# First parameter load ahead of the gate weights, a fixed VectorE order in the head, one engine per transpose copy, and the column matmuls ahead of tile 2

## The chip, the cores and the metric

The kernel runs on one NeuronCore of one Trainium2 chip. The metric is device time in microseconds; the time of a kernel is the median of its runs. The engines are TensorE (PE), VectorE (DVE), ScalarE (ACT), GpSimd (POOL) and SyncE (SP); SP and ACT also issue the DMAs. The trace calls SP's DMA queue q1 and ACT's q10.

## The reference

One layer on x of 2048 tokens by 448 features, in bf16. It normalizes each token, sends the result through a diagonal complex state-space scan (branch A) and a gated MLP (branch B), and joins the two:

```python
xn = _layernorm(x, axis=-1)
# branch A: dt = exp(log_dt); Lam_bar = exp(dt*Lam); B_bar = ((Lam_bar-1)/Lam)[:,None]*B
#   Bu = xn @ B_bar.T ; h_t = Lam_bar*h_{t-1} + Bu_t ; s = 2*Re(h @ C.T) + xn*Dskip
# branch B: (sigmoid(xn @ w_gate) * (xn @ w_up)) @ w_down, w_gate and w_up 448 x 1792
return x + s * silu(branch_B)
```

Lambda_re, Lambda_im and log_dt are vectors of 448; they are called "the parameters" below.

## The kernel before, in words

**Tiling.** The 2048 tokens are 16 tiles of 128, worked in four chunks of 512 tokens. The features stay on the partitions: `xnT` holds a chunk of the normalized x transposed, as 7 blocks of 64 features by 512 tokens. For each chunk, 14 steps (`gu_step`, L683) make 7 gate and 7 up blocks. In chunk 0 the seven gate blocks come first and then the seven up blocks, and from chunk 1 on they alternate. The matmuls of a step (L662, L663) go in pairs on the two halves of the array. ACT takes tanh of a gate block (L676), and DVE multiplies it with the up block (L679) into `hF`. `b_units` (L692) makes the scan's input, `ssm_pair` and `ssm_stack` (L753, L789) do the scan on DVE, `down` (L823) is the second MLP matmul, and `yout` (L841) is the scan's output matmul with the last three DVE operations (L861, L863, L865) and the store.

**The head.** The work of chunk 0 that the change touches is this. x tiles 0 to 3 are loaded one by one, tiles 0 and 2 from SP and 1 and 3 from ACT (L372 to L375). The gate weights come as four transfers. The first 256 columns of each half (blocks 0 and 1; 224 KB each) go out at L376 on SP and L377 on ACT, and the other 640 columns (blocks 2 to 6; 560 KB each) at L382 on SP and L379 on ACT. Below they are "the small" and "the large" gate-weight transfers. The three parameter rows (`load_p`, 0.9 KB each) go out on SP between them (L378, L380, L381). Then SP loads x tiles 4 to 7 in one transfer (L383), half of the up weights (L895), the skip row `dbc` (L896) and the transposed B matrices (L601).

For tiles 0 to 3, DVE computes statistics (`stats`, L395, L396), ACT the square root (L404), POOL a copy of the mean (L405), and DVE the reciprocal (L406) and the normalized tile (`norm`, L418). PE transposes each tile into a PSUM bank (`pe_transpose`, L450 to L452). For tiles 0 and 1 the bank is copied out by ACT (4 of 7 blocks, L455) and DVE (3 blocks, L457) together, and for tiles 2 and 3 by DVE alone (L460). `columns` (L486) turns the three parameter rows into columns with five small matmuls (L492, L494), DVE copies them out (`pv`, L498), and POOL works out `turn` and `r` from them (L506 to L515). The sine tables (`tables`, L522) start from `turn`. On PE the head runs: 11 warm-up matmuls, transposes of tiles 0 and 1, two warm-up matmuls, gate block 0 of tiles 0 and 1, transposes of tile 2, gate block 1 of tiles 0 and 1, transposes of tile 3, the columns, then gate block 2 of tiles 0 and 1. That last one needs both large transfers.

**What sets the order.** Operations are not issued as written. `Plan.add` (L82) records each with an engine, a cost and its dependencies. `Plan.solve` (L132) works out a latest start for each backwards from PE's written order, and then runs all engines forward, taking on each engine the ready operation with the earliest latest start; `emit` (L222) writes the instructions in the order of the planned starts. PE operations keep the written order (L102), and so do DMAs and others added with `chain=True`. DVE, ACT and POOL operations may change places whenever a cost or a planned time changes, anywhere in the kernel. A fixed order of 16 tiles in four chunks thus comes out of the costs that are written in the code.

**The DMA counters.** The DMAs from SP and ACT take eight completion counters in turn, and a DMA that reuses a counter waits at issue until the DMA eight places before it has landed. The planner has the same rule:

```python
k = len(landed)
if k >= 8:
    o.end = free[e] = max(o.end, landed[k - 8] + o.cost)
```

In the issued order of the kernel before, the large SP gate-weight transfer is the eleventh DMA and the small one on SP the third. So the large one waits for the small one to land, and the instructions after it in SP's queue wait behind it. The large one on ACT is the tenth and waits for x tile 2, the second.

Of the kernel before, what the change touches and what calls it, by code (L numbers as in the profile page):

```python
# [20 lines left out]
P = 128  # L21
H = 64
# [50 lines left out]
class Plan:  # L73
# [3 lines left out]
    def __init__(self, horizon):  # L77
        self.ops, self.w, self.r = [], {}, {}
        self.horizon = horizon
        self.last_of = {}  # L80

    def add(self, eng, cost, fn, r=(), w=(), dma=0, lat=None, chain=False, name="", rate=230e3):  # L82
# [19 lines left out]
        if chain or eng == "PE":  # L102
# [29 lines left out]
    def solve(self, pe_from):  # L132
# [58 lines left out]
        while todo:  # L191
# [13 lines left out]
            if o.dma:  # L205
                if e == "POOL":
                    o.lat = 6.0
                else:
# [3 lines left out]
                    q = dma_free[e] = max(dma_free.get(e, 0.0), o.end + 1.2) + o.dma / o.rate  # L212
                    o.lat = q + 0.8 - o.end
# [14 lines left out]
def kernel(  # L228
# [113 lines left out]
    def load_w(eng, k, half, b, r=()):  # L342
# [5 lines left out]
             wsrc[k][:, c0 + m0 * P:c0 + m1 * P].rearrange("(s p) f -> p s f", p=H), cost=0.65, r=r, rate=145e3)  # L348
# [26 lines left out]
    load_x(3, 1, "ACT")  # L375
    load_w("SP", "g", 0, 0)  # L376
    load_w("ACT", "g", 1, 0)  # L377
    load_p("SP", 0)  # L378
    load_w("ACT", "g", 1, 1)  # L379
    load_p("SP", 1)  # L380
# [12 lines left out]
    def stats(t):  # L393
        b = t % 3
        add("DVE", 0.53, lambda: V.bn_stats(out=bst[b][:], in_=x_all[:, t, :]), r=[("x", t)], w=[("bst", b)])  # L395
        add("DVE", 0.1, lambda: V.bn_aggr(out=mv[:, t, :], in_=bst[b][:]), r=[("bst", b)], w=[("mv", t)])  # L396

    def chain(t0, n):
# [4 lines left out]
        if t0 < TPC:  # L403
            add("ACT", 0.2, lambda: A.activation(sd, var, ACT.Sqrt, bias=epsc[:]), r=ks("mv") + ["sqrttab", "epsc"], w=ks("sd"))  # L404
            add("POOL", 0.15, lambda: G.tensor_copy(out=meanf[:, t0:t0 + n, :], in_=mean), r=ks("mv"), w=ks("mf"))  # L405
            add("DVE", 0.09, lambda: V.reciprocal(out=rs, in_=sd), r=ks("sd"), w=ks("rs"))  # L406
# [8 lines left out]
    def norm(t):  # L415
        b = t % NXN
        if t < TPC:
            add("DVE", 0.33, lambda: V.tensor_scalar(out=xn[b][:, 0:448], in0=x_all[:, t, :],  # L418
# [25 lines left out]
    def pe_transpose(t):  # L444
# [9 lines left out]
        if t < 2:  # L454
            add("ACT", 0.5, lambda: A.copy(out=xnT[0][:, 0:4, js], in_=tp[:, 0:4, :]),  # L455
                r=[("acc", a)], w=[("xnT", 0, t, "a")])
            add("DVE", 0.27, lambda: V.tensor_copy(out=xnT[0][:, 4:7, js], in_=tp[:, 4:7, :]),  # L457
                r=[("acc", a)], w=[("xnT", 0, t, "b")])
        else:
            add("DVE", 0.53, lambda: V.tensor_copy(out=xnT[0][:, :, js], in_=tp[:, :, :]),  # L460
# [419 lines left out]
    for t in range(4):  # L880
        stats(t)
        chain(t, 1)
        norm(t)
    slots0 = [next_gu() for _ in range(3)]

    pe_transpose(0)
    pe_transpose(1)
    warm_mm(2)
    gu_mm(0, "g", 0, slots0[0], 0, 2, True)
    pe_transpose(2)  # L890
    gu_mm(0, "g", 1, slots0[1], 0, 2, True)
# [147 lines left out]
```

## Time and profile before

| | |
|---|---|
| runs | 195.15, 193.25, 196.12, 196.08, 193.71 us; median 195.15 us |
| profiled execution | 195.15 us, of which the span of the trace is 193.4 us |
| busy, share of span | PE 94%, DVE 88%, ACT 44%, POOL 18% |
| DMA | 13.41 MB; 5.9 to 9.9 tenths busy in the first five slices, little afterwards |
| first gate matmul | 7.49 us; gate block 2 of tiles 0 and 1 starts at 13.72 us |
| mean granted PE clock | 0.987 over the span |

Times in the profile are counted from the start of the span. A PE that is shown busy need not be at its peak, since ends of matmuls are modelled. An engine's "idle before" and the waits name what came last before an instruction could start. The page's second part cuts the span into 40 slices of 4.83 us. In the row PEclk a 9 stands for the full clock.

### The profile page before, as it was taken

What the parts mean: (1) busy time and instruction counts of PE and PEld (TensorE: products, weight loads), DVE (VectorE), ACT (ScalarE), POOL (GpSimd) and SP (SyncE); (2) the same over time, 40 slices, a digit from 0 to 9 for tenths busy, and PEclk for the clock granted to TensorE, in tenths of its full rate; (3) what the DMA queues carried; (4) which work ended last, traced back from release to release, by engine and by line L of the source; (5) the groups of instructions that cost most, each with busy time, mean ns of one, the idle gap of its engine ahead of it and who ended that gap; (6) DMA issues with size and microseconds to landing.
All of it is one profiled execution on the core that took longest, in us unless ns stands there. A gap on an engine that the chain in (4) does not pass through costs nothing.

```text
span 193.4 us, 3453 instructions
## 1 busy us (share of the span) xinstructions
PE 181.2 (94%) x1340; PEld 87.5 (45%) x1347; DVE 170.3 (88%) x310; ACT 84.4 (44%) x117; POOL 34.1 (18%) x92
## 2 busy tenths in 40 slices
PE   7759999999999999999989999999989999999990
PEld 2447444444445444454435444444435444455550
DVE  3827879999999999999999999999999999992074
ACT  3515996473967835134477321244346151112100
POOL 3136583400002670000355200000000000000000
PEclk9996999999999999999999999999999999999998
DMA  5999934599300024200013410000001000101011
GB/s 143 221 237 283 166 73 98 123 333 185 124 0 3 0 47 90 56 0 0 3 29 92 96 26 24 0 27 0 24 0 51 0 0 0 54 24 47 0 42 53
DMA packets 28310, 13.41 MB, mean 69 GB/s; under 512 B 19587, under 2 KB 28294, under 8 KB 28294
## 3 DMA queue, kind: packets, MB, share of 16 engines
q1 hardware_dynamic: 26614, 11.36, 25.8%
q10 hardware_dynamic: 1680, 1.84, 3.9%
q8 instruction: 10, 0.16, 0.4%
q14 instruction: 6, 0.05, 0.1%
HBM read 6.77 MB, written 1.84 MB: 44 GB/s over the span
## 4 chain that ended last, share of the span: by engine, by line
DVE 55%; PE 28%; issue 7%; DMA 6%; POOL 2%; ACT 1%; SPq 0%; DVEq 0%; POOLq 0%
DVE hF L679 13%; PE gu L662 13%; DVE wv L769 8%; DMA wG<-in_B_w_gate_dram 6%; PE gu L830 5%; PE acc L855 4%; PE acc L830 4%; DVE ta L762 3%; DVE tb L763 3%; DVE z L765 3%; DVE o_t L861 3%; DVE tb L784 3%; DVE ta L783 3%; DVE hT L786 2%; DVE o_t L863 2%
## 5 line engine op out<-in xcount | busy, mean ns | idle before, releaser
L662 PE MATMUL gu<-xnT,wG 64*128 64x512 bf16 (+1 forms) x217 | 48.0, 367 | 2.2 <-DMA wG<-in_B_w_gate_dram 2.1
L663 PE MATMUL gu<-xnT,wG 64*128 64x512 bf16 (+1 forms) x217 | 48.0, 367 | 0.0
L662 PE MATMUL gu<-xnT,wU 64*128 64x512 bf16 x196 | 46.1, 376 | 0.0
L663 PE MATMUL gu<-xnT,wU 64*128 64x512 bf16 x196 | 46.1, 376 | 0.0
L676 ACT ACTIVATE sig<-gu 128x1024 f32<-128x1024 f32 x21 | 21.5, 1023 | 36.7 <-PE gu L663 36.5
L830 PE MATMUL acc<-wd,hF 128*128 128x448 bf16 x168 | 33.8, 353 | 0.0
L662 PEld LDWEIGHTS <-wG 64*128 64x128 bf16 x217 | 20.6, 98 | 24.8 <-issue 2.6
L830 PEld LDWEIGHTS <-hF 128*128 128x128 bf16 x224 | 21.5, 98 | 21.3 <-issue 2.1
L662 PEld LDWEIGHTS <-wU 64*128 64x128 bf16 x196 | 18.0, 94 | 23.6 <-issue 2.1
L679 DVE SCALAR_TENSOR_TENSOR hF<-sig,gu 128x1024 bf16<-128x1024 f32 x21 | 25.3, 1207 | 0.0
L769 DVE TENSOR_TENSOR_SCAN wv<-c_r,st,z 128x512 bf16<-128x512 f32 x18 | 23.0, 1276 | 0.0
L855 PE MATMUL acc<-cT,hT 128*128 128x448 bf16 x105 | 21.8, 353 | 0.0
L663 PEld LDWEIGHTS <-wG 64*128 64x128 bf16 x217 | 20.5, 98 | 0.3 <-issue 0.2
L663 PEld LDWEIGHTS <-wU 64*128 64x128 bf16 x196 | 18.0, 94 | 0.0
L726 ACT CAST bus<-gu 128x1024 bf16<-128x1024 f32 x12 | 12.1, 1011 | 12.8 <-PE gu L715 12.8
L861 DVE TENSOR_TENSOR o_t<-acc,xd 128x448 bf16<-128x448 f32 x15 | 9.2, 614 | 9.2 <-PE acc L855 9.2
L715 PE MATMUL gu<-xnT,bT 128*128 128x512 bf16 x65 | 15.3, 379 | 1.1 <-issue 1.1
L855 PEld LDWEIGHTS <-hT 128*128 128x128 bf16 x119 | 11.5, 98 | 10.1 <-issue 0.4
L836 ACT ACTIVATE g_t<-acc 128x448 bf16<-128x448 f32 x12 | 6.4, 537 | 18.3 <-PE acc L830 18.3
L395 DVE BATCH_NORM_STATS2 bst<-x_all 128x6 f32<-128x448 bf16 x16 | 9.4, 614 | 5.5 <-DMA x_all<-in_A_x_dram 5.5
L409 POOL TENSOR_SCALAR veb<-mv 128x2 bf16<-128x2 bf16 x6 | 2.5, 410 | 49.7 <-DVE mv L396 49.5
L830 PE MATMUL gu<-wd,hF 128*128 128x448 bf16 x56 | 10.8, 352 | 0.0
(131 smaller groups left out, 242.2 us busy)
## 6 DMA issues: line engine op xcount, KB each, us to landing
out_dram<-o_t SPq DMA_DIRECT2D x15, 112.0 KB, 1.7
wd<-in_B_w_down_dram SPq DMA_DIRECT2D x1, 1568.0 KB, 7.3
x_all<-in_A_x_dram SPq DMA_DIRECT2D x3, 448.0 KB, 6.5
wU<-in_B_w_up_dram SPq DMA_DIRECT2D x1, 784.0 KB, 12.4
wU<-in_B_w_up_dram ACTq DMA_DIRECT2D x1, 784.0 KB, 13.3
wG<-in_B_w_gate_dram ACTq DMA_DIRECT2D x1, 560.0 KB, 6.1
wG<-in_B_w_gate_dram SPq DMA_DIRECT2D x1, 560.0 KB, 7.3
xnT<-xn SPq DMA_TRANSPOSE x24, 2.4
```

The costliest lines, as they stand in the source:

```text
L395: add("DVE", 0.53, lambda: V.bn_stats(out=bst[b][:], in_=x_all[:, t, :]), r=[("x", t)], w=[("bst", b)])
L662: T.matmul(gu[a][:, 0, ts], lhsT=w_[0:H, s, ms], rhs=x[0:H, s, ts], start=(s == 0), stop=(s == 6))
L663: T.matmul(gu[a][:, 1, ts], lhsT=w_[H:P, (s + 1) % 7, ms], rhs=x[H:P, s, ts], start=(s == 0), stop=(s == 6))
L676: add("ACT", act(1024), lambda: A.activation(th, gu[a][:], ACT.Tanh, scale=0.5), r=[("gu", a)], w=[tk])
L679: add("DVE", dve1(1024), lambda: V.scalar_tensor_tensor(out=ho, in0=th, scalar=1.0, in1=gu[a][:], op0=ALU.add, op1=ALU.mult), r=[("gu", a) ...
L715: T.matmul(gu[a][:, i, :], lhsT=bT[:, kt, i, pt * P:pt * P + P], rhs=x[:, 2 * kt, :], start=False, stop=(kt == 2))
L726: add("ACT", act(1024), lambda u=u, a=a: A.copy(out=bus[u][:], in_=gu[a][:]), r=[("gu", a)], w=[("bus", u)])
L769: dve(1.194, lambda k=k: V.tensor_tensor_scan(out=wv[:, k, :], data0=rb, data1=z[:, k, :], initial=(st[pt][:, k, :] if c else 0.0), op0=AL ...
L830: T.matmul(d, lhsT=hF[c % 2][:, m, h, js], rhs=wd[:, ft, :], start=(ft == 0), stop=(ft == FT - 1))
L836: add("ACT", act(448), lambda: A.activation(g_t[g][:], d, ACT.Silu, scale=0.5), r=[key, "silutab"], w=[("gt", g)])
L855: T.matmul(y, lhsT=hT[c % 2][:, hm, js], rhs=cT[:, cm, c0:c1], start=(i == 0), stop=(i == 6))
L861: add("DVE", dve1(n), lambda od=od, y=y, c0=c0, c1=c1: V.tensor_tensor(out=od, in0=y, in1=xq[:, c0:c1], op=ALU.add), r=[key, ("xd", q)], w ...
```

## The change

It has six parts.

1. The first parameter row's load is moved on SP ahead of the small gate-weight transfer. On each queue the other loads keep their order. In the issued order of the changed kernel the parameter row is the third DMA, the small SP gate-weight transfer is the fifth, and the large one is still the eleventh. Its counter is now that of the parameter row. The up weights on SP now wait for the small gate weights, and `dbc` for the small ACT transfer.
2. While `pl.seq` is set, from the first statistics to the `dbc` load, DVE operations are chained in written order.
3. That written order is: statistics of tiles 0 and 1, reciprocal and norm of 0 and of 1, statistics of 2, copy of tile 1, statistics of 3, reciprocal and norm of 2 and of 3, `pv`, copies of tiles 2 and 3.
4. Tile 0's transpose is copied out whole by ACT, tile 1's whole by DVE. One ACT instruction and one DVE instruction fewer remain, each longer.
5. On PE, gate block 1 of tiles 0 and 1 and then the columns come before the transposes of tile 2.
6. Costs in the planner change: DMA latencies 1.2 to 0.9 and 0.8 to 0.6 us, the gate-weight rate 145 to 135 GB/s, and DVE and ACT costs of the head's operations upwards.

As a consequence of the last, the order on DVE, ACT and POOL changes in many places after the head too. On DVE, the first reads of PSUM of about eight `yout` steps (L861) stand one to four places earlier, and updates L679, scans L769 and table operations trade places with neighbours. On POOL, three operations of `coeffs` (L564, L570, L564) come before the first `veb` (L409). PE's order changes only in the head, and SP's by the parameter row and one swap of a transposing DMA.

```diff
@@ Plan.__init__
         self.last_of = {}
+        self.seq = False
@@ Plan.add
-        if chain or eng == "PE":
+        if chain or eng == "PE" or (eng == "DVE" and self.seq):
@@ Plan.solve
-                    q = dma_free[e] = max(dma_free.get(e, 0.0), o.end + 1.2) + o.dma / o.rate
-                    o.lat = q + 0.8 - o.end
+                    q = dma_free[e] = max(dma_free.get(e, 0.0), o.end + 0.9) + o.dma / o.rate
+                    o.lat = q + 0.6 - o.end
@@ load_w
-             ... cost=0.65, r=r, rate=145e3)
+             ... cost=0.65, r=r, rate=135e3)
@@ loads
     load_x(3, 1, "ACT")
+    load_p("SP", 0)
+    load_w("ACT", "g", 1, 0)
     load_w("SP", "g", 0, 0)
-    load_w("ACT", "g", 1, 0)
-    load_p("SP", 0)
+    load_p("SP", 1)
     load_w("ACT", "g", 1, 1)
-    load_p("SP", 1)
     load_p("SP", 2)
     load_w("SP", "g", 0, 1)
     load_x(4, 4)
@@ stats, chain, norm: costs only
-0.53, 0.1 (bn_stats, bn_aggr); 0.2 (Sqrt), 0.09 (reciprocal), 0.33 (norm)
+0.6, 0.16; 0.3, 0.2, 0.42
@@ pe_transpose
-        if t < 2:
-            add("ACT", 0.5, lambda: A.copy(out=xnT[0][:, 0:4, js], in_=tp[:, 0:4, :]), ...)
-            add("DVE", 0.27, lambda: V.tensor_copy(out=xnT[0][:, 4:7, js], in_=tp[:, 4:7, :]), ...)
+        if t == 0:
+            add("ACT", 0.85, lambda: A.copy(out=xnT[0][:, :, js], in_=tp[:, :, :]), ...)
         else:
-            add("DVE", 0.53, lambda: V.tensor_copy(out=xnT[0][:, :, js], in_=tp[:, :, :]), ...)
+            add("DVE", 0.64, lambda: V.tensor_copy(out=xnT[0][:, :, js], in_=tp[:, :, :]), ...)
@@ the head
     warm_mm(11)
-    for t in range(4):
-        stats(t)
+    pl.seq = True
+    stats(0)
+    stats(1)
+    for t in (0, 1):
         chain(t, 1)
         norm(t)
+    stats(2)
     slots0 = [next_gu() for _ in range(3)]
     pe_transpose(0)
     pe_transpose(1)
+    stats(3)
+    for t in (2, 3):
+        chain(t, 1)
+        norm(t)
     warm_mm(2)
     gu_mm(0, "g", 0, slots0[0], 0, 2, True)
+    gu_mm(0, "g", 1, slots0[1], 0, 2, True)
+    columns()
     pe_transpose(2)
-    gu_mm(0, "g", 1, slots0[1], 0, 2, True)
     pe_transpose(3)
     silu_table()
     load_w("ACT", "u", 1, 0, r=["silutab"])
     load_w("SP", "u", 0, 0)
     load("SP", "dbc", P * D * 2, dbc[:], A_Dskip.unsqueeze(0).to_broadcast((P, D)))
-    columns()
+    pl.seq = False
```

## The prediction

> **What bounds the kernel now.** I read the chain of waits first. It begins with two DMAs, one behind the other, and only then comes to an engine (columns: start, duration, what):
>
> ```profile
> 0.72 0.39 SPq L333
> 1.17 0.42 SPq L333
> 1.63 4.72 DMA wG<-in_B_w_gate_dram
> 6.37 7.31 DMA wG<-in_B_w_gate_dram
> 13.72 0.28 PE gu L662
> ```
>
> The small gate-weight transfer on SP lands at 1.63 + 4.72 = 6.35 us; the large one is issued at 6.37, lands at 13.68, and gate block 2 starts at 13.72. SP's own waits show why it went out so late:
>
> ```profile
> SPq L333 <- DMA wG<-in_B_w_gate_dram: 2.8, 1, 2.8
> ```
>
> SP was done with its fifth DMA at 3.27 + 0.25 = 3.52 and then stood for 2.8 us until the small transfer had landed: the wait for a completion counter. The waits of the compute engines from 0 to 30 us name the victims (columns: total, times, longest):
>
> ```profile
> DVE bst L395 <- DMA x_all<-in_A_x_dram: 5.5, 2, 3.4
> PE gu L662 <- DMA wG<-in_B_w_gate_dram: 2.1, 1, 2.1
> ```
>
> DVE's 3.4 us are the wait for x tiles 4 to 7, which stand behind the large transfer in SP's queue and are used from 15.55. Next, the stretches of the head (columns: stretch, length, busy of PE, PEld, DVE, ACT and POOL, granted clock, DMA share, GB/s):
>
> ```profile
> 9.00:12.00 3.00, 2.45 (x35) 1.73 (x35) 1.82 (x6) 1.22 (x1) 0.00 (x0) 1.00 1.08 223
> ...
> 13.70:15.00 1.30, 1.28 (x16) 1.01 (x18) 0.00 (x0) 0.00 (x0) 1.06 (x4) 0.68 1.08 221
> 15.00:17.00 2.00, 2.00 (x23) 1.46 (x20) 1.45 (x3) 0.46 (x1) 0.96 (x3) 0.50 1.05 333
> 17.00:18.50 1.50, 1.50 (x26) 1.23 (x24) 1.50 (x6) 1.17 (x2) 1.03 (x2) 0.81 1.10 281
> ```
>
> Two things are to be seen. PE, once it has its weights, works at half clock for a while after 13.7. And the DMA engines count as fully busy everywhere, but move 223 GB/s in one stretch and 333 in another. The packet records by queue tell the two apart: in 9 to 12 us nearly all packets are SP's, in 15 to 17 SP and ACT have about half each. What comes after the head is the last view, stretches and waits from 14 us on:
>
> ```profile
> 48.00:72.00 24.00, 23.84 (x173) 11.24 (x174) 23.94 (x41) 17.59 (x26) 7.57 (x12) 1.00 0.12 38
> ```
> ```profile
> PE gu L705 <- DVE hF L679: 1.2, 2, 0.8
> ```
> ```profile
> DVE o_t L861 <- PE acc L855: 9.2, 1, 9.2
> ```
>
> PE and DVE are both full. PE waits hardly at all; at the end DVE waits 9.2 us for PE. So after 13.72 the kernel is one unbroken run of PE with DVE in step beside it, and a start that is x earlier for both is an end that is x earlier.
>
> **What the Trainium skill says.** "DMA: Bandwidth & Descriptors", section "Queues, rings and completion order": SP and ACT each have a ring of their own on every DMA engine, and descriptors of one ring are taken in order. The trace agrees: the 0.9 KB log_dt row, issued at 2.41 behind the small transfer, has its landing record at 6.55 us, after that transfer's. The same page, "Issuing engines are not separate DMA queues", says that issuing from several engines saves issue time only, since all run on the same 16 engines. Taken strictly, an earlier issue would then gain only what the engines had idle. The 223 against 333 GB/s speak against it here, and I follow the measurement. "TensorE: Matmul & The Clock Gate", Part 1: a free-running window of about 3.4 us; after an idle window the PE clock is halved. The trace agrees: two gate blocks at half clock of some 3.4 us length, after 2.1 us without a matmul.
>
> **The change part by part.**
>
> *Parameter row first.* The eleventh DMA, the large SP transfer, now takes the counter of the parameter row. That row sits behind x tiles 0 and 2 only; their landing records end at 3.15 and 3.71 us, so it lands at about 3.8. SP is done with its other issues at about 3.55. The large transfer goes out at about 3.9, not 6.37. It costs the small transfer one issue of 0.50 us: about 6.7 instead of 6.35, hidden, since the first gate matmul (7.49) waits for the transposes' copies and the ACT half lands at 7.06 anyway. The other two rows still go behind the small transfer (records 6.80 and 7.35), before the columns need them.
>
> When do both large transfers land? The ACT one starts to move at about 5.6 us (packet records). From there both rings are busy with 1120 KB. At 333 GB/s (1120 KB x 1.024 / 333 = 3.4 us) they are through at 9.0, and the slowest of the 16 engines, which was 1.0 to 1.7 us behind its fellows for SP's large transfers, at 10.0 to 10.7. If two rings gain nothing, only the hole counts: in 5.5 to 6.5 us 150 GB/s moved instead of 223, 0.3 us, and they land at 13.3. Later than 13.68 is excluded, as nothing but 0.9 KB came ahead of them. I take 10.6.
>
> *PE's path to gate block 2.* Gate block 0 starts as before: ACT's copy of tile 0 runs from 6.24 and lasts 0.91 (estimate: between 0.59 for 512 and 1.01 for 1024 elements of the casts at L730 and L726) to 7.15; DVE's copy of tile 1 (0.62, as at L460) from 6.86 to 7.48. Then 0.8 + 0.8 for blocks 0 and 1, the columns 0.3, to 9.4; tile 2's norm ends near 8.8 (it was 9.14), so its transposes run 9.4 to 9.9. Tile 3's need the bank that `pv` frees; that is one DVE copy of 0.17 at 9.55, and they end at 10.4. So PE is ready at 10.4, the weights come at 10.6: block 2 starts 3.1 us earlier. The fixed order and the whole copies hide behind the weights; they are worth little alone, but if they failed, each 0.1 us late on this path would cost 0.1. `pv` waits for PE with tile 2's copy queued behind it: 0.2 us, covered by the transposes.
>
> *Half clock.* From 13.72 to the first up block at 24.50 are 10.8 us. The work is four half blocks of 7 x 0.109 and four whole ones of 7 x 0.216 = 9.1. So 1.7 us were lost to the clock. With a pause below 0.3 us there is nothing left to trip it: gain 1.7, bounds 0 and 1.7 (with weights at 12 or later, likely 0).
>
> *Up weights.* PE would reach them at 24.5 - 3.1 - 1.7 = 19.7. They landed at 8.63 + 13.3 = 21.9, behind everything else in the queues. The two rings side by side save 4.8 (1120 KB at 240) less 3.4 = 1.4 us, the hole 0.3; and ACT's half starts sooner because SP's backlog does. I take 1.8: landing at 20.1, so PE gives 0.4 back. (Bounds: 0 to 2.2 given back.)
>
> *DVE.* x tiles 4 to 7 landed at 15.53. Behind a large transfer that is 3 us earlier they land near 12.5. `turn` is ready at `pv` 9.7 + 1.8 (11.95 to 13.92, less the copy) = 11.5, so the first table operation (0.47) fills the wait. From 15.55 to the first up update at 26.27 DVE did 9.5 us of work; now 9.0 from 12.5: 21.5, which is 4.8 earlier, about where PE's first up block (20.1 + 1.5) is. Two waits stand in the way: `xd` needs `dbc`, which landed at 22.0 just as DVE came to it, and L606, now one place earlier, needs the B transposes. With DMA only 1.8 to 2.5 us ahead and DVE 3 to 3.5, I take 0.7 us for both (0 to 1.5).
>
> *Rearranged middle.* The same operations in nearly the same places. I take 0, bounds -1 and +6 (rival 3).
>
> Sum: 3.1 + 1.7 - 0.4 - 0.7 = 3.7. The profiled execution took 195.15 (span 193.4), as much as the median: 191.4.
>
> **The rivals.**
>
> 1. *Engine-bound DMA.* If 16 busy engines are the limit and not the rings, the large transfers share rather than overlap and land near 12.5 to 13.3. For: DMA share 1.08 in the single-ring stretch, and the skill's sentence. Against: 333 GB/s at share 1.05. Half clock stays. Gain 0.8 to 1.2: 194.1.
>
> 2. *Given back to DVE.* The head gains, but `dbc`, L606 and the up weights keep their old times, so DVE's first update is only 2 us earlier, and DVE, full to 172, sets the pace. For: the SP queue runs without a pause from 9.3 to 35.6 us. Gain 2: 193.1.
>
> 3. *Slower.* The place is DVE's order after 70 us. The page on TensorE says under "Architectural detail" (queue depths) that DVE is strictly first in, first out. About eight L861, which read `yout`'s bank, now stand one to four places earlier, ahead of L679 or L769. If PE has not finished, DVE stands, the update behind it comes late, and PE waits for the bank that it would free. One `yout` takes PE 1.32 us (chain: seven matmuls at L855); 0.8 each is 8 x 0.8 = 6.4 lost, less 3.7: 197.9. It decides for slower than before once the waits exceed 0.46 each. Against: before, no L861 before 172 us waited noticeably on PE.
>
> That the change does nothing, because the row lands late after all, ends like rival 1.
>
> **How the numbers follow.** Forecast 0.60 (191.4; its bounds 190 to 192.8), rival 1 0.19 (194.1), rival 2 0.14 (193.1), rival 3 0.07 (197.9). About 1%, 2 us, is what a measurement of this kernel tells from no change: faster is below 193.2. From the forecast 0.58, rival 2 0.08 and rival 1 0.04 make 0.70 faster; rival 3 0.07 slower; the rest, 0.23, is same. The range 189.9 to 195.0 leaves out rival 3 and a tenth at most beside it.
>
> **What would show it.** In the profile after: the large SP transfer issued near 3.9 us; gate block 2 at 10.4 to 10.8 with no wait above 0.3; full clock in slice 4; x tiles 4 to 7 used near 12.5; the first up matmul near 20.1; DVE's first L679 near 22; no new wait on L855 before the end. I am wrong if block 2 still starts after 12.5, if the half clock is there again, or if DVE shows waits for PE at L861 in the middle.

## The result and the profile after

| | before | after |
|---|---|---|
| median of all executions | 195.36 us (193.0 to 197.32, 80) | 195.37 us (192.34 to 204.94, 43) |
| ratio to before, 95% interval | | 0.9956 [0.9932, 0.998] |
| profiled execution, its span | 195.15, 193.4 us | 192.97, 191.2 us |
| first matmul of gate block 2 | 13.72 | 12.11 (its other half: 13.92) |
| first use of x tiles 4 to 7 | 15.55 | 15.10 |
| first up matmul | 24.50 | 22.92 |
| first up update (before L679, after L678) | 26.27 | 24.79 |

The medians of all executions are equal. The ratio compares only executions within 1.5% of the fastest of their kernel, which leaves out more than half of after's (24 of 44, the profiled one counted). By this ratio the change gains 0.44%, 0.86 us of 195.4; the longer executions of after, up to 204.94 us, give it back. The forecast was 3.7 us, and 191.4 us.

First the chain of waits of after, its head (start, duration, what). Line numbers are one higher than before's ahead of `pe_transpose` and one lower behind it.

```profile
3.73 0.60 SPq L334
4.37 10.70 DMA x_all<-in_A_x_dram
15.10 0.64 DVE bst L396
...
18.41 0.58 POOL veb L410
19.06 1.08 POOL sdb L411
20.21 1.65 POOL rsd L412
...
22.99 0.76 ACT xn L424
23.75 0.91 ACT hF L675
...
28.01 1.21 DVE hF L678
```

The large SP gate transfer went out at 3.73 us, as predicted (3.9). It is no longer the thing that the chain hangs on. x tiles 4 to 7 go out right behind it, at 4.37, and take 10.7 us to land: they are used at 15.10, 0.45 us earlier than before, though they were issued 2.65 us earlier (4.37 against 7.02). (Traces in which these transfers are issued alike differ by more than 0.45 us here, as the table behind e2 shows.) From them the chain runs over the statistics, five POOL operations of the second group's norm, and a norm step on ACT, which stands in ACT's queue ahead of a tanh. The waits from 0 to 32 us (total, times, longest):

```profile
ACT hF L675 <- PE gu L662: 5.3, 2, 5.1
...
DVE bst L396 <- DMA x_all<-in_A_x_dram: 4.4, 2, 2.3
...
PE gu L662 <- DMA wG<-in_B_w_gate_dram: 1.5, 1, 1.5
...
PE gu L661 <- DMA wG<-in_B_w_gate_dram: 0.6, 1, 0.6
```

PE waits twice for gate block 2 now: 0.6 us for SP's half and 1.5 us for ACT's, 2.1 in all, exactly as much as before in one piece. The wait did not go; the two transfers changed places. Before, ACT's landed at 9.85 and SP's at 13.68 (landing records). After, SP's lands at 12.07 and ACT's at 13.87. A gate block needs both.

On SP's queue the wait for a landing is 2.1 us, not 2.8, and now stands ahead of the up weights, as the diff says:

```profile
SPq L334 <- DMA wG<-in_B_w_gate_dram: 2.1, 1, 2.1
```

The stretches (stretch, length, busy of PE, PEld, DVE, ACT, POOL, granted clock, DMA share, GB/s):

```profile
9.00:12.00 3.00, 2.53 (x41) 1.87 (x35) 2.09 (x6) 1.53 (x2) 1.41 (x3) 1.00 1.13 258
...
13.70:15.00 1.30, 1.08 (x20) 0.98 (x22) 0.00 (x0) 0.00 (x0) 1.15 (x4) 1.00 1.10 215
15.00:17.00 2.00, 2.00 (x41) 1.77 (x39) 1.86 (x5) 1.35 (x2) 0.45 (x2) 1.00 1.04 277
17.00:18.50 1.50, 1.50 (x19) 1.30 (x15) 1.50 (x5) 1.50 (x2) 0.09 (x1) 1.00 1.68 264
...
48.00:72.00 24.00, 23.84 (x179) 11.19 (x180) 23.63 (x42) 17.82 (x27) 8.93 (x14) 1.00 0.18 50
```

From 9 to 12 us both rings are at work, and they move 258 GB/s at a share of 1.13: 16% above the 223 of one ring, where I had reckoned with 333. The half clock is absent from this execution: 1.00 in all stretches. In the middle PE and DVE are as full as before. Of the two waits shown before, PE's for an update has shrunk from 1.2 to 0.5, and DVE's for PE is still the one wait at the end:

```profile
DVE o_t L860 <- PE acc L854: 8.6, 1, 8.6
...
PE gu L704 <- DVE hF L678: 0.5, 1, 0.5
```

The two profiled executions differ by 2.2 us. The head gives 1.5 of it (first update 26.27 to 24.79). The rest is 0.7: from the first update to the end of the span, before takes 167.1 and after 166.4. But the medians of all executions are equal, and the ratio gives 0.86, so the pair of profiles flatters the change.

One figure holds in all seventeen profiles of this document, whatever was changed. From the third up update to the end of the span they take 163.0 to 164.9 us, while that update starts anywhere between 26.66 us (e13) and 36.74 us (e1). The head decides when the kernel ends, as the prediction had it. The first update alone can mislead: in e3 and e7 it is early (24.69 and 24.12), but the third waits for ACT and starts at 29.48 and 28.70.

### The profile page after: what moved, and what is told of

Its sections match the earlier page's. It is cut to its first block, busy times and chain, and to the rows that moved or that the text cites. A ratio compares the mean times of both kernels' runs of the same rounds, so it can differ in the third digit from the quotient of the medians.

```text
span 191.2 us, 3457 instructions
## 1 busy us (share of the span) xinstructions
PE 180.2 (94%) x1340; PEld 93.3 (49%) x1347; DVE 170.4 (89%) x309; ACT 83.9 (44%) x116; POOL 34.5 (18%) x92
## 2 busy tenths in 40 slices
DMA packets 28310, 13.41 MB, mean 70 GB/s; under 512 B 19587, under 2 KB 28294, under 8 KB 28294
## 4 chain that ended last, share of the span: by engine, by line
DVE 56%; PE 21%; DMA 7%; issue 6%; POOL 5%; ACT 3%; SPq 1%; DVEq 0%; POOLq 0%
DVE hF L678 13%; DVE wv L768 9%; DMA x_all<-in_A_x_dram 6%; PE gu L661 6%; PE gu L829 6%; PE acc L854 4%; PE acc L829 4%; DVE ta L761 3%; DVE tb L762 3%; DVE o_t L860 3%; DVE z L764 3%; DVE bst L396 3%; DVE tb L783 2%; DVE hT L785 2%; ACT xn L424 2%
## 5 line engine op out<-in xcount | busy, mean ns | idle before, releaser
L662 PE MATMUL gu<-xnT,wG 64*128 64x512 bf16 (+1 forms) x217 | 46.3, 356 | 1.5 <-DMA wG<-in_B_w_gate_dram 1.5
L661 PE MATMUL gu<-xnT,wG 64*128 64x512 bf16 (+1 forms) x217 | 46.4, 356 | 1.0 <-DMA wG<-in_B_w_gate_dram 0.6
L829 PE MATMUL acc<-wd,hF 128*128 128x448 bf16 x168 | 33.8, 353 | 0.0
L661 PEld LDWEIGHTS <-wG 64*128 64x128 bf16 x217 | 19.8, 94 | 19.8 <-issue 3.0
L678 DVE SCALAR_TENSOR_TENSOR hF<-sig,gu 128x1024 bf16<-128x1024 f32 x21 | 25.1, 1201 | 0.0
L662 PEld LDWEIGHTS <-wG 64*128 64x128 bf16 x217 | 19.8, 94 | 2.7 <-DMA wG<-in_B_w_gate_dram 1.7
L860 DVE TENSOR_TENSOR o_t<-acc,xd 128x448 bf16<-128x448 f32 x15 | 9.2, 612 | 8.6 <-PE acc L854 8.6
L854 PEld LDWEIGHTS <-hT 128*128 128x128 bf16 x119 | 11.5, 98 | 10.1 <-issue 0.4
## 6 DMA issues: line engine op xcount, KB each, us to landing
wU<-in_B_w_up_dram SPq DMA_DIRECT2D x1, 784.0 KB, 12.4
wU<-in_B_w_up_dram ACTq DMA_DIRECT2D x1, 784.0 KB, 13.5
```

What stands on the lines that cost most here:

```text
L661: T.matmul(gu[a][:, 0, ts], lhsT=w_[0:H, s, ms], rhs=x[0:H, s, ts], start=(s == 0), stop=(s == 6))
L662: T.matmul(gu[a][:, 1, ts], lhsT=w_[H:P, (s + 1) % 7, ms], rhs=x[H:P, s, ts], start=(s == 0), stop=(s == 6))
L678: add("DVE", dve1(1024), lambda: V.scalar_tensor_tensor(out=ho, in0=th, scalar=1.0, in1=gu[a][:], op0=ALU.add, op1=ALU.mult), r=[("gu", a) ...
L829: T.matmul(d, lhsT=hF[c % 2][:, m, h, js], rhs=wd[:, ft, :], start=(ft == 0), stop=(ft == FT - 1))
L854: T.matmul(y, lhsT=hT[c % 2][:, hm, js], rhs=cT[:, cm, c0:c1], start=(i == 0), stop=(i == 6))
L860: add("DVE", dve1(n), lambda od=od, y=y, c0=c0, c1=c1: V.tensor_tensor(out=od, in0=y, in1=xq[:, c0:c1], op=ALU.add), r=[key, ("xd", q)], w ...
```

## The experiments

Three readings were to be told apart. One: the 16 DMA engines, not the issue, set when the gate weights land. Two: the clock is what the head gains or loses. Three: a gain at gate block 2 is taken away by the next late thing, above all the up weights, of which ACT's half goes out close to SP's first transposing DMA (B matrices). All ratios are to runs of the kernel before on the same chip; the figures in brackets are 95% intervals.

**The two halves of the change.** *e1* is before with only the first parameter row and the small SP gate transfer exchanged:

```diff
-    load_w("SP", "g", 0, 0)
+    load_p("SP", 0)
     load_w("ACT", "g", 1, 0)
-    load_p("SP", 0)
+    load_w("SP", "g", 0, 0)
```

The planner's entries keep their places and costs here and in e2, so no other instruction moves. (The diffs show what is loaded, not the planner's entries.)

> The kernel before with the two first SP transfers exchanged (parameter row ahead of the small gate weights), all else in the order of before. Theory A (the order of the transfers decides, and x tiles 4 to 7 now share the engines with ACT's large gate weights): SP's large transfer is issued near 3.8 us and lands by 12.5, ACT's lands last near 13.7, gate block 2 of tiles 0 and 1 starts at 13.4 to 14.0, x tiles 4 to 7 are used 0.4 us or more earlier than 15.55; time within 0.5 us of before. Rival (the load move is worth what I forecast and something in the rest took it back): block 2 starts before 12, time 2 us or more below before.

Measured: 1.0019 [0.9989, 1.0049], median 197.21 (194.33 to 202.51). The profiled execution is the longest one, 202.51. Its waits, and its DMA issues by SP and ACT from the up weights on (timeline: start, duration, queue):

```profile
PE gu L665 <- DMA wU<-in_B_w_up_dram: 6.3, 1, 6.3
```
```profile
6.46 0.61 SPq L333 DMA_DIRECT2D wU<-in_B_w_up_dram  x1
...
7.90 9.54 SPq L351 DMA_TRANSPOSE bT<-in_A_B_re_dram  x1
...
9.27 0.60 ACTq L333 DMA_DIRECT2D wU<-in_B_w_up_dram  x1
```

The large transfer went out at 3.89 and landed at 14.22, so gate block 2 gained nothing (14.27). And SP, freed early, came to its first transpose at 7.90, 1.37 us ahead of ACT's half of the up weights. That half landed at 30.0; before it went out 0.67 us ahead of the transpose and landed at 21.96. PE stood 6.3 us for it.

*e2* is after with the same two transfers put back, so the order alone:

```diff
     load_x(3, 1, "ACT")
-    load_p("SP", 0)
+    load_w("SP", "g", 0, 0)
     load_w("ACT", "g", 1, 0)
-    load_w("SP", "g", 0, 0)
+    load_p("SP", 0)
```

> The changed kernel with the first two SP transfers put back in the order of before. Theory A: SP's large transfer is issued near 6.4 us and lands near 13.7 as before; the measured 0.4% lies in the order of VectorE and TensorE, so the time stays 0.4 to 1 us below before. Rival (the gain is in the load move): time equals before within 0.3 us.

Measured: 0.9946 [0.9902, 0.999], median 194.75. The large transfer went out at 6.52 again, gate block 2 began at 12.96, the first update at 25.51 (before 26.27), and from there to the end it took 166.3 us (before 167.1). So the order alone measures as much as the whole change, and the part that I priced at 3.1 us adds nothing to it. If anything it costs: the longest of e2's 14 executions took 195.37 us, which 21 of after's 43 exceed. The earlier start of gate block 2 in e2's profile is not the order's doing, since SP's large transfer, issued as late as in before, happened to take 6.39 us instead of 7.31. Which part of the order gains (the VectorE order, the copies, the place of the columns, or what the costs move later on) was not separated.

The landings say the same. In nine traces SP issues the parameter rows, and the gate weights come in full on two rings. In before, e2, e6 and e12 the parameter row has its old place, and in after, e1, e4, e5 and e8 it goes first:

| | old place (4 traces) | row first (5 traces) |
|---|---|---|
| large SP gate transfer issued | 6.37 to 6.57 | 3.73 to 4.01 |
| last of the two large transfers landed | 12.91 to 13.96 | 13.41 to 14.44 |
| x tiles 4 to 7 used | 14.48 to 15.84 | 15.10 to 16.86 |

An issue that came 2.4 to 2.8 us earlier brought no earlier landing. e1 shows one way in which this happens. From 7 to 10 us its two rings moved the gate weights and the first of x tiles 4 to 7 at the rate of the forecast:

```profile
7.00:10.00 3.00, 2.10 (x27) 1.25 (x24) 1.98 (x8) 1.97 (x5) 0.36 (x2) 1.00 1.01 330
```

But a transfer has landed only with the last of its 16 landing records, which the prediction reads as one for each engine. Of SP's large transfer fifteen had come by 11.96 and the last came at 14.22; of ACT's, by 11.70 and at 13.96. e4 and e8 show it for ACT's as well: half of its records had come by 10.35 and 9.38, and the last at 14.14 and 13.42. Packets of x tiles 4 to 7 were moving from 9 us on by then, and packets of the up weights from 10. In after it went differently. From 6 to 8 us SP's ring was nearly alone (206 GB/s), and all records of ACT's large transfer came late, from 12.55 to 13.87.

**Who overtakes the up weights.** *e8* is e1, and *e5* is after, each with ACT's half of the up weights issued by SP in the place of the skip row `dbc`, ahead of the transposes, and `dbc` by ACT:

```diff
-    load_w("ACT", "u", 1, 0, r=["silutab"])
+    load("ACT", "dbc", P * D * 2, dbc[:], A_Dskip.unsqueeze(0).to_broadcast((P, D)), r=["silutab"])
     load_w("SP", "u", 0, 0)
-    load("SP", "dbc", P * D * 2, dbc[:], A_Dskip.unsqueeze(0).to_broadcast((P, D)))
+    load_w("SP", "u", 1, 0)
```

> The load move alone (as in the first of these kernels: parameter row ahead, the rest as before), with both halves of the up weights on SP ahead of the B transposes. Theory C: the slow executions of the load move alone (199 to 202) are gone, median 195.0 to 195.5, no wait for wU. Rival D: median 197 and executions up to 202 as there.

> The changed kernel with ACT's half of the up weights and the skip row exchanged: SP issues both halves of the up weights ahead of the B transposes, ACT loads the skip row. Theory C (the load move lets SP issue the B transposes ahead of ACT's half of the up weights, whose landing then sets the first up matmul): both halves have landed by 21.5 us in every execution, no wait of TensorE for wU, executions within 3 us of each other, median 193.5. Rival D (the spread of the changed kernel comes from the clock and from the chip, not from the up weights): median 195.4 and the same spread as the changed kernel.

e8: 0.9954 [0.992, 0.9987], median 194.52; no wait for the up weights, and the executions of e1 up to 202.51 are gone: nine of e1's 22 took over 199 us, and the longest of e8's 14 took 197.97. What e8 gains by its ratio is not to be seen in its profile, where the first update starts at 26.40 (before 26.27). e5: 1.0022 [0.9985, 1.0059], median 195.31. No wait for the up weights, and the tail is gone (204.94 to 197.57), but the 0.44% is gone too: in its profile the half clock is back, and the first update is at 25.85 instead of 24.79. So the overtaking explains the tails. It does not explain e5's ratio.

*e6* is before with the first transpose issued ahead of `dbc`:

```diff
-    load("SP", "dbc", P * D * 2, dbc[:], A_Dskip.unsqueeze(0).to_broadcast((P, D)))
+    tload([("bT", 0)], bT[:, 0:3, 0, :], A_B_re[:, 0:384], D * 768)
...
-            tload([("bT", i)], bT[:, 0:3, i, :], m[:, 0:384], D * 768)
+            if i == 0: load("SP", "dbc", P * D * 2, dbc[:], A_Dskip.unsqueeze(0).to_broadcast((P, D)))
+            else: tload([("bT", i)], bT[:, 0:3, i, :], m[:, 0:384], D * 768)
```

> The kernel before with the first B transpose ahead of the skip row on SP, so that it is issued near 8.4 us, ahead of ACT's half of the up weights (8.6). Theory C: that half lands at 23 us or later instead of 21.96, in some executions far later, and the median rises by 1 us or more, with a spread of over 5 us as in the load move alone. Rival D: no change from before beyond 0.3 us.

Measured: 1.0081 [1.0053, 1.0108], median 196.57, with no long tail. Of its waits up to 32 us the longest that is new:

```profile
DVE xd L431 <- DMA dbc<-in_A_Dskip_dram: 3.4, 1, 3.4
```

The victim is not the up weights but the 112 KB of `dbc`, which landed at 25.1 instead of 22.0, so that the first update came at 28.70. On SP's queue the reason is the issue itself (timeline: start, duration, queue):

```profile
8.39 9.33 SPq L900 DMA_TRANSPOSE bT<-in_A_B_re_dram  x1
17.77 0.57 SPq L602 DMA_DIRECT2D dbc<-in_A_Dskip_dram  x1
```

The transpose held SP for 9.33 us, and `dbc` went out at 17.77 instead of 8.35. ACT's half of the up weights, issued 0.42 us behind the transpose on the other queue, took 15.1 us instead of 13.3, and PE waited 0.5 us for it. So in this kernel what comes behind the first transpose is late on both queues: on SP's because it is issued late, on ACT's because it lands slowly.

How a transfer on the other queue slows down shows in the packet records, KB in each microsecond by queue (SP's q1 + ACT's q10; T marks packets of 256 bytes, which appear with the transposing DMAs):

```
us       before         after          e1
15-16    138 + 140      116 + 103      173 + 32  T
16-17    177 + 196      133 + 189       79 + 88  T
17-18     95 + 193 T     84 + 193 T     40 + 84  T
18-19     55 + 173 T     56 + 145 T     19 + 51  T
19-20     52 + 32  T     36 + 61  T     13 + 11
```

Until the transposing packets begin, the sum is 219 to 373 KB per us; after that it falls to between 24 and 97 by 19 to 20. By 19 us 629 of the 784 KB of ACT's half had moved in after, which landed at 22.42, and 255 in e1, which landed at 30.0. What is left of a transfer by then crawls. e8 shows that the order against the transposes matters; whether their packets slow the others, or SP's long issue of them (7.5 us for the first in before, 9.5 in e1), was not separated.

**The gate transfers on one ring.** *e3* is after with ACT's large gate transfer issued by SP, just ahead of SP's own:

```diff
-    load_w("ACT", "g", 1, 1)
+    load_w("ACT", "g", 1, 1, via="SP")
```

> The changed kernel, with the large gate-weight transfer of ACT issued on SP just ahead of SP's own, so that x tiles 4 to 7 follow both in one ring. Theory A (x tiles 4 to 7 and the up weights took half of the engines from the late gate weights): both large transfers have landed by 11.7 us, gate block 2 starts near 12.0, x tiles 4 to 7 are used at 14 or earlier, time 2 us below the changed kernel. Rival B (sixteen busy engines cannot deliver the gate weights before 13.3, whatever the order): block 2 at 13.3 or later, time as the changed kernel.

Measured: 0.99 [0.9851, 0.9948], six executions. *e10* is the same kernel again, with more of them:

> The one-ring kernel once more (both large gate-weight transfers on SP ahead of x tiles 4 to 7), for its time. Theory B: block 2 at 13.0 again, x tiles 4 to 7 used later than 15.1, so little is won: 194.5, 0.4% below before, within the interval of the changed kernel. If the first run's ratio of 0.990 holds, the median is 193.5.

0.9894 [0.9867, 0.9921], median 194.45. In e3's profiled execution, the longest of its six (196.19), the large transfers landed at 10.0 and 13.0, one behind the other; in e10 gate block 2 began at 13.62, no earlier than before, with the half clock. SP had one more large issue ahead of the transposes, and ACT's half of the up weights went out 1.0 (e3) and 1.65 us (e10) ahead of them. With the load moved and the transfers on two rings it went out 0.34 (after), 0.66 (e4) and 1.37 us (e1) behind them. That this lead makes the gain is not shown, and *e7* speaks against it. It is e3 with both halves of the up weights on SP as in e5, so it has them safe as well:

> Both large gate-weight transfers on SP (as in the one-ring kernel) and both halves of the up weights on SP ahead of the B transposes. Theory C: block 2 at 13.0 as in the one-ring kernel, up weights by 21.5, median 193.0, 2.4 us below before, and the fastest of all. Rival D: as the one-ring kernel, 193.5, with its spread.

0.9985 [0.9957, 1.0013]. By the ratio it gains nothing. PE had its up weights by 22.34, and a DVE update, the third, waited for ACT:

```profile
DVE hF L678 <- ACT cosT L540: 1.5, 1, 1.5
```

**The clock.** *e4* is after and *e12* before, both with eight warm-up matmuls ahead of gate block 2, so that PE isn't idle there:

```diff
         def f():
+            for _ in range(8 if (c, k, m, lo, hi) == (0, "g", 2, 0, 2) else 0):
+                T.matmul(gu[a][:, 0, :], lhsT=warm[:, 0:P], rhs=warm[:], start=True, stop=True)
             for s in range(7):
```

> The changed kernel with eight more warm-up matmuls on TensorE ahead of gate block 2 of tiles 0 and 1, in the time in which it waits for weights. Theory A (the runs differ by whether the clock is halved after that pause): the granted clock is full from 6 us to the end, the runs lie closer together, and the median falls by 1 us or more. Rival (the halved clock costs nothing, since VectorE sets the pace): no change in the median.

> The kernel before with eight more warm-up matmuls on TensorE in its pause ahead of gate block 2. In the trace of before the clock was halved from 14.2 to 17.6 us and the first up matmul came at 24.5, 2.5 us after the up weights. If the halved clock costs what I forecast, the clock is full after 4 us, the first up matmul comes at 22.8 to 23.2, and the median falls by 1 to 1.7 us to 194. Rival F: full clock, first up matmul near 23, but the first update of VectorE and the end hardly move (0.5 us or less), as ScalarE's norms of x tiles 4 to 7 and VectorE hold it.

e4: 0.9982 [0.995, 1.0015]. e12: 1.0007 [0.9972, 1.0042]. In both profiled executions the clock was full through the head. In e12's profile the first up matmul came 1.3 us earlier (23.21), the first update 0.7 earlier (25.53), and the executions gained nothing. In e4, ACT's half of the up weights landed at 24.97, and PE waited 1.0 us for it.

The other executions can be told apart by their mean granted clock. In the seventeen profiles it is 0.975 to 0.991 where the half clock appears ahead of the end, and 0.992 or more where it does not. By this mark none of e12's 14 executions had the half clock, and 19 of the 35 of before on the same chip had it. A full clock worth 1.7 us would then have gained about 0.9 us (estimate: 19/35 of 1.7), and the interval allows 0.55 at most. So the full clock alone is worth less than I had put it at, and nothing that can be measured here.

**The parameter rows by another queue.** *e11* is after with the three rows issued by GpSimd:

```diff
-    load(eng, ("vrow", k), ..., cost=0.25)
+    load(eng, ("vrow", k), ..., cost=0.25, via="POOL")
```

> The changed kernel with the three parameter rows issued by GpSimd, so that they use no counter of SP's and ACT's DMAs: both large gate-weight transfers go out without any wait, by 3.0 us. Theory A (issue time and order decide): both land by 11.5, block 2 starts at 11.5 to 12.2, time 193. Theory B: they go out at 3 us and still land at 12.8 to 13.9, block 2 in the same stretch, time within 0.5 us of the changed kernel.

Measured: 1.0225 [1.0153, 1.0297], six executions. Both large transfers were issued at 2.4 us. The first half of gate block 2 began at 12.41, the other, for which ACT's transfer landed at 13.39, at 13.44. The waits:

```profile
PE gu L662 <- DMA wU<-in_B_w_up_dram: 4.2, 1, 4.2
```

SP was at its first transpose by 7.05; ACT's half of the up weights went out at 12.09, since ACT came late to that place in its order, and landed at about 27. With the large transfers issued 1.3 and 2.0 us ahead of after's, gate block 2 had both halves 0.3 us earlier than in before (13.44 against 13.72), and the transposes began 2.25 us earlier (7.05 against 9.30).

**Fewer bytes.** *e9* is after with the large gate transfers cut from 560 to 224 KB each. They carry blocks 2 and 3 only, and blocks 4 to 6 of the gate use the weights of blocks 2 and 3:

```diff
-             wgt[k][ps, :, m0 * P:m1 * P], ...
+             wgt[k][ps, :, m0 * P:cut(k, m1) * P], ...    # cut: gate blocks up to 4
-        ms = slice(m * P, m * P + P)
+        mw = 2 + m % 2 if k == "g" and m > 3 else m
+        ms = slice(mw * P, mw * P + P)
```

> The changed kernel with the two large gate-weight transfers cut from 560 to 224 KB each: blocks 4 to 6 of the gate are computed with the weights of blocks 2 and 3, and nothing else is left out. 672 KB fewer ahead of everything that follows. Theory B (the DMA engines' rate sets when the head's data lands, and the order of issue does not): both large transfers land by 11.5 us, gate block 2 starts as soon as TensorE is ready (11.3 to 12.2), x tiles 4 to 7 are used 2 to 3 us before 15.1, the up weights land 2 to 3 us earlier, and the time falls by 2 to 3 us below the changed kernel: 192.8. Rival F (an earlier head is given back later, since VectorE or ScalarE sets the pace after it): the landings move as said, but the time stays within 0.7 us of the changed kernel.

Gate block 2 began at 10.83 and x tiles 4 to 7 were used at 12.14: the numbers that I had forecast for the change (10.6 and 12.5). PE was at the up weights at 19.95 (forecast 19.7). And the kernel took 200.69 us, 1.0268 [1.0227, 1.0309]. The waits and the chain:

```profile
PE gu L666 <- DMA wU<-in_B_w_up_dram: 7.9, 1, 7.9
```
```profile
8.33 19.84 DMA wU<-in_B_w_up_dram
28.17 0.05 issue
28.21 0.60 PE gu L666
```

With fewer bytes both large transfers landed by 9.62. And SP, yet earlier at its transposes (7.82), had passed ACT's half of the up weights (8.33), which took 19.84 us. *e13* is e9 with both halves of the up weights on SP, as in e5:

> The kernel with fewer gate bytes (the two large gate transfers carry blocks 2 and 3 only; gate blocks 4 to 6 use the weights of blocks 2 and 3, so 672 KB less are moved and the output differs), and in addition both halves of the up weights on SP ahead of the transposed B matrices, dbc on ACT. Theory U (the end was lost to up weights that the transposes passed, and nothing else stands behind it): gate block 2 near 10.8, no wait for the up weights above 1 us, first up matmul near 20, first update near 22 to 23, which is 2 to 3 us earlier than in the changed kernel: median 192 to 193.5, ratio 0.985 to 0.99. Theory V (another limit is within 1 us behind: x tiles 4 to 7, statistics, the norm chain on POOL and ACT): gate block 2 near 10.8 again, first update not before 24, ratio 0.993 to 1.0, and the waits name the chain. A ratio above 1.01 would say that the transposes were not the cause.

190.77 us, 0.9779 [0.9728, 0.9831]: 4.3 us faster than before. Gate block 2 at 11.04, x tiles 4 to 7 at 12.97, the first up matmul at 20.24 without a wait, the first update at 23.64, and full clock throughout. Its chain hangs on `dbc` next, for which DVE waited 1.6 us:

```profile
8.53 12.21 DMA dbc<-in_A_Dskip_dram
20.75 0.02 issue
20.77 0.39 DVE xd L435
...
23.64 1.21 DVE hF L682
```

So with landing times near those of my forecast and the up weights safe, the end does come earlier, by 4.3 us where my sum said 3.7. That the two are close is in part luck: the first update came 2.6 us earlier where I had about 4.3 (near 22), 0.9 us were gained behind the third update, where I had nothing, and 672 KB less are on the engines.

**The same with everything computed.** *e14* and *e15* are after with both halves of the up weights on SP and each large gate transfer split: blocks 2 and 3 (224 KB) where the large one stood, blocks 4 to 6 (336 KB) behind. In e14 ACT still issues its parts; in e15 SP issues all, in the order of need, with x tiles 4 to 7 between the two groups:

```diff
-    BLK = {"g": [(0, 2), (2, 7)], "u": [(0, 7)]}
+    BLK = {"g": [(0, 2), (2, 4), (4, 7)], "u": [(0, 7)]}
-    load_w("ACT", "g", 1, 1)
+    load_w("SP", "g", 1, 1)          # e14: "ACT"
     load_p("SP", 2)
     load_w("SP", "g", 0, 1)
     load_x(4, 4)
+    load_w("SP", "g", 1, 2)          # e14: "ACT"
+    load_w("SP", "g", 0, 2)
```

> The changed kernel with both up halves on SP ahead of the transposes, and each large gate transfer split in two: blocks 2 and 3 (224 KB) where the large one stood, blocks 4 to 6 (336 KB) behind x tiles 4 to 7 (SP) and directly behind the first part (ACT). Everything is computed. Theory N (what counts is the bytes ahead of gate block 2): block 2 near 11 to 11.5, block 4 waits under 0.5 us, up weights used by 21.5 to 22.5, ratio 0.98 to 0.99. Theory M (the bytes altogether set the time of the up weights, and PE gives back there what it gains): block 2 at 11 to 12 but a wait of 1.5 us or more for the up weights or for the skip row, ratio 0.992 to 1.002. x tiles 4 to 7 share the engines with ACT's second part, so I expect them at 13.5 to 14.5.

> The same, with all gate transfers after the two small ones on SP in the order in which they are needed: blocks 2 and 3 of both halves, x tiles 4 to 7, blocks 4 to 6 of both halves, both up halves. Theory N: block 2 at 10.5 to 11.5, x tiles 4 to 7 at 12.5 to 13.5, block 4 without a wait above 0.5, ratio 0.975 to 0.985, better than with two rings. Theory M: same head, then a wait for the up weights (1120 + 448 KB and 1568 KB at the 223 KB per us of one ring from 4 us end at 18 and then 25 us less what the halves overlap), first update not before 25, ratio 0.992 to 1.002.

e15: 192.64 us, 0.9888 [0.9832, 0.9943], six executions, with e3's kernel the best that computes everything. Gate block 2 began at 11.64, x tiles 4 to 7 were used at 12.29, and the first up matmul came at 20.76, with a wait of 0.6 for the other half just behind it. But the first update came at 24.59, hardly earlier than after's. The chain says why:

```profile
13.43 1.05 POOL c_r L507
...
16.39 0.50 POOL veb L412
16.96 1.01 POOL sdb L413
...
20.00 0.76 ACT xn L426
20.75 0.91 ACT hF L677
```
```profile
DVE spm L545 <- ACT spm L540: 1.3, 1, 1.3
```

POOL works at the scan's coefficients until 16.39 before it takes up the norm of x tiles 4 to 7. ACT's norm step at 20.00 holds back two tanhs and, behind them, a sine for which DVE waits 1.3 us just ahead of the update. Up to there most of what I had forecast is gained (10.6, 12.5 and 20.1 were the figures); the next limit costs most of it again. This is read from the chain of one execution. In e14 and e15 the order on DVE, ACT and POOL changes in some places too, and both up halves go out ahead of the transposes, so that e15's gain is not that of the order of the loads alone.

e14: 1.0061 [1.0031, 1.0091], and nothing about DMAs can be learned from its time. Its waits:

```profile
DVE bst L398 <- DMA x_all<-in_A_x_dram: 6.1, 2, 3.9
...
PE acc L453 <- DVE pv L499: 3.8, 1, 3.8
```

With other planned landing times the planner put the statistics of x tile 4 on DVE ahead of the column copy `pv`. DVE stood 3.9 us for the tile, PE 3.8 for the copy, and gate block 2 began at 15.81.

## Why the prediction was wrong, by its own steps

**Parameter row first: the issue was right, the landing wrong.** "They are through at 9.0, and the slowest of the 16 engines at 10.0 to 10.7" is the step that failed. The two large transfers had landed at 13.87 in after and at 13.41 to 14.44 in all five traces with the row first, so its 3.1 us were 0. Two terms of it were mis-sized. The rate: 333 GB/s was read from a stretch in which both rings carried up weights, and after moved 206 from 6 to 8 us, with SP's ring nearly alone, and 258 from 9 to 12. The slowest engine: I had put it 1.0 to 1.7 us behind its fellows, and in e1, where the rate was there (330 GB/s from 7 to 10 us), half of the landing records of both transfers had come by 10.6 and the last at 14.22, 3.6 us later. The rate alone would not have saved the forecast. Further, the sum counted 1120 KB and left out the 448 KB of x tiles 4 to 7, which the same early SP queue put on the engines at 4.37. The bound "later than 13.68 is excluded" was also wrong: it was drawn from SP's transfer, and ACT's, which had landed at 9.85, came to be the last at 13.87. The Trainium skill's "DMA: Bandwidth & Descriptors", section "Issuing engines are not separate DMA queues", says that issue from several engines saves the issue and no more, since all run on the same 16 engines. I had set a measurement against that. For the landings the sentence holds in all five traces; for the rate it is not settled here, since two rings moved from 16% (after) to 48% (e1) more than the 223 of one.

**Half clock: right in one trace by luck, and not in the time.** The pause was as long as before, yet the profiled execution kept the full clock: what I derived from a shorter pause came about without one, and e5 with the same pause had the half clock. By the mean clock, as for e12, the profiled execution is one of few: 34 of after's 44 executions had the half clock, against 78 of the 191 of before that were taken beside the experiments. The ten of after without it have a median of 193.34 us, the others 195.76. That is no measure of what the clock costs, since a long wait brings the half clock too (e1's profile has it from 27.0 to 33.8, during and behind its wait of 6.3 us). e12 had the full clock and gained nothing, so PE's time in the gate blocks was not alone the end of the path. "TensorE: Matmul & The Clock Gate", Part 1, has a window of about 3.4 us that runs free; where it lies against the pause may differ from one execution to the next, which would fit, but no run shows it. The prediction found page and trace in agreement; the 3.4 us of half clock agree, but the page asks for an idle window of about 3.4 us ahead of it, and the pause was 2.1.

**Up weights: wrong.** I put them at 20.1. SP's half came at 19.54, ACT's at 22.42, and in e1's longest execution at 30.0. The step followed only the queue's backlog and not what SP does with the time it is given: it issues its transposes sooner, and those slow what is behind them. I had followed the completion counters that the move touches, and not the transposes behind them.

**DVE: wrong with its input.** The 12.5 for x tiles 4 to 7 was 15.10. Where they did land near it (12.97 in e13), the first update came at 23.64; I had said 22.

**The copies, and the middle.** ACT's whole copy took 0.91 as estimated, DVE's 0.62. But PE, which I had ready for gate block 2 at 10.4, was ready at 11.5 in after (before 11.6), and began it at 10.83 in e9, where no weights were late. This cost nothing as long as the weights came last. The middle, taken as 0 with bounds -1 and +6, gained 0.7 us in the profile (167.1 to 166.4 from the first update to the end); with the same order it is 166.3 in e2, but 167.1 in e4 and e10, so the gain is not steady. Rival 3 did not occur: no L860 waits for PE before the end.

**The rivals.** Rival 1, engine-bound DMA, came nearest: an earlier issue without an earlier landing, and the half clock still there in most executions. Its number (194.1; the ratio gives 0.9956 x 195.15 = 194.3) was met for another reason: its gain of 0.8 to 1.2 us was to come from the load, and e2 shows that it comes from the order. I gave it 0.19. Rival 2 had part of it: the up weights (22.42 against 21.96) and `dbc` (21.53 against 22.03) did keep their old times.

**Open.** Why e5 is not faster than before, while e8, the same exchange on e1, is by its ratio; what the one-ring kernel of e3 and e10 gains by; how the executions of one kernel come to differ by 5 us; why one of a transfer's 16 landing records comes so late; and what besides the number of rings decides between 220 and 370 KB per us (e13 moved 302 between 7 and 8 us with rows of 512 and 896 bytes, after 217 to 264 from 8 to 11 with rows of 896 and 1280).

## What to carry to other kernels

Issuing a transfer earlier helps only if the DMA engines have room: count all bytes that are under way at that time, on all queues, against a rate measured in that stretch, and ask which transfer, and which of its landing records, becomes the last. Then follow the queue that was freed to its next instructions, since what it issues sooner may overtake something that is needed first; here PE waited up to 7.9 us for what transposing DMAs had overtaken. Sending first what is used first, on one ring and all ahead of the transposes (e15), measured 1.1% where an earlier issue gained nothing; how much of this is the order of the loads was not separated. And compare more than one trace of each kernel: the same transfer, issued at the same time, landed up to 1 us apart in traces of kernels that differ elsewhere.

## What the runs showed of the hardware that was not expected

- A plain transfer that is still under way when transposing DMAs begin slows down greatly: 784 KB took 20.7 us in e1 and 19.84 in e9, against 12.4 to 13.5 us in before and after. Both queues together fell to 24 KB per us in e1 between 19 and 20 us, at a busy share of 0.07 of the plain and transposing packets' own records, so the engines were not kept busy by the packets that the trace shows.
- Issuing a transposing DMA can hold SP's queue for 7.5 us (before) to 9.5 us (e1), and all that stands behind it goes out that much later.
- The last of a transfer's 16 landing records can come long after the fifteenth: 2.3 us for both large gate transfers in e1 (11.96 to 14.22, 11.70 to 13.96), against 0.1 us for ACT's and 1.0 for SP's in before.
- The rate of two rings side by side is not one number: 258 GB/s in after from 9 to 12 us, 330 in e1 from 7 to 10 with the same gate weights, 333 in before with up weights.
